# A linear-attention block and an MLP on one core: shorter warming, half of a block's reciprocal loads on ScalarE's queue, two more DMA transposes, and a new order

## The chip, the core and the metric

The kernel runs on one core of a Trainium2 chip. The core has TensorE (PE: matrix products, with its weight loads shown apart as PEld), VectorE (DVE), ScalarE (ACT), GpSimd (POOL) and SyncE (SP), which here only issues DMAs. Each engine works through its own queue in order, and semaphores between the queues make an instruction wait for what it reads or overwrites. Products land in PSUM, whose eight banks of 128 x 512 floats are one tile, `bk`.

The metric is device time in microseconds (us), median of several executions. The profile is of one execution, and its times count from the start of the profiled span.

## The reference, cut to what matters

All is bfloat16 outside; S = 2048 rows, D = 512, 32 heads of 16, Dff = 1792.

```python
n = layernorm(x)
q, k, v = split_heads(n @ wqkv)
phi = lambda t: where(t > 0, t + 1, exp(t)) + 1e-6
pq, pk = phi(q), phi(k)
kv = einsum("bhsd,bhse->bhde", pk, v)        # sums over all 2048 rows
z  = einsum("bhsd->bhd", pk)
o  = einsum("bhqd,bhde->bhqe", pq, kv) / (einsum("bhqd,bhd->bhq", pq, z)[..., None] + 1e-6)
h  = x + o_as_rows @ wo
out = h + maximum(layernorm(h) @ w1, 0) @ w2
```

`kv` and `z` need every row, so the attention's second half can't begin before the last row tile's `pk` is there.

## The kernel before

The 2048 rows are 16 row tiles of 128 (t), in 4 blocks of 512 columns after transposition (c = 0 to 3; c = 0 is block 1 of the title). The program is one list of words, `ORDER` (lines 18 to 54). Each word calls one small function, `op_<name>`, with the numbers behind the dots, and issues that function's instructions. Nothing else decides the order: an engine's queue is the list cut down to the words of that engine.

The words that matter here, by stage:

- `warm.n.b.w` (line 243): n products of zeros, w columns wide, before there is data.
- `lx`, `lk`, `lq`, `lv`, `lo`, `l1`, `l2`: loads of row tiles and weights, on SP. `l1` and `l2` of 896 KB bring the two halves of w1 and w2.
- `S.t`, `A.t` (lines 248, 249, DVE): statistics of row tile t; `R` (254, 255, ACT): the reciprocal root; `N.t` (262, DVE): the normalised rows.
- `T.t` (287, PE) transposes by four products, `E.t` (297, ACT) copies the result to `lnT`. For tiles 5 to 15 `X.t` (308, SP) does it with one DMA transpose.
- `K.t.b` (316, PE) is k of a row tile in bank b, four products of 512 columns; `K.t.b.k.n` does n of the four from k. `Q.c.j.b` (324, PE) is a quarter of q of block c. Behind either: exp (`F`, `qF`; line 334, ACT), relu (`U`, `qU`; 337, ACT), `M`/`qM` (341, DVE) and the addition `D`/`qD` (344, DVE).
- `G.t` (368, PE) sums n^T pk over the rows into banks 4 to 7; `za`, `zf`, `zhi`, `zlo` (DVE) sum pk, and `z` (392, PE) turns the sums to columns. The k of the last tiles goes straight into `z`, which so needs the last `D`.
- `zc`, `zh` (DVE), then `d4.c` (440, PE): the denominators of block c; `dl4`, `dx4` (446, 451, ACT): their reciprocals by log and exp. `wb.c` (468, SP) writes them to DRAM, and eight `rb.c.h` (471, SP; 64 KB each) read them back spread over the rows of one buffer, `rr`. `dm.c` (484, DVE) multiplies pq by them, into `pqs`.
- `gA`, `gD` (406, 409) copy the sums G out; `kv` (414, PE), `kx` (422, DVE, into `kvbd`), `m` (426, PE), `mA`, `mD` (429, 432): the weights of the second half, `m_sb`.
- `h.t` (493, PE), `hD.t` (499, DVE): h of a row tile, with the residual. `s`, `a` (250, 251, DVE): its statistics; `n.t` (270, DVE) or `nA.t` (276, ACT) subtracts the mean (with the sign turned); then `x.t` (309, SP) transposes by DMA. Tiles 2 and 3 have instead `t.t` (287, PE) and `v.t` (306, DVE).
- `p.c.f` (508, PE): 128 columns of the hidden layer for a block, four products; `ph.c.f.b.half` (517) the same for half of the block's rows; `pA`/`pD` (523, 528) the relu. `f.t.b.f0.n` (537, PE) the last products of a row tile, `fo` (545, DVE) the sum with h, `fd` (552, SP) the store.

Two rules set waits in all stages: a bank is overwritten only when its readers are through, and `rr`, `eb` and `rb` are used again in the same way.

Of the kernel before, what the change touches and what calls it, by code (L numbers as in the profile page):

```python
# [15 lines left out]


ORDER = """
table const masks warm.70.7.64 warm.2.7 lx.0.1 S.0 A.0 R.0.1 lx.1.1 S.1 lx.2.1 A.1 N.0 T.0.1 lk.0.4 S.2 R.1.1
N.1 T.1.2 lx.3.1 A.2 E.0 K.0.4 R.2.1 lx.4.2 S.3 N.2 T.2.1 E.1 A.3 S.5 R.3.1 K.1.0.0.2 K.1.0.2.2 N.3 S.4 A.5 A.4  # L20
E.2 T.3.2 K.2.6.0.2 K.2.6.2.2 F.0.1 M.0.1 lx.6.2 E.3 S.7 lq.0.4 R.4.2 lx.8.4 Q.0.3.1 N.4 U.0.1 A.7 F.1.1 F.2.1
T.4.2 N.5 S.6 Q.0.1.4 U.1.1 M.1.1 A.6 lx.12.4 M.2.1 D.0.1 R.6.2 K.3.7.0.2 K.3.7.2.2 E.4 X.5 U.2.1 U.3.1 D.1.1
N.6 Q.0.0.3 N.7 S.10 qF.0.0.2 K.4.5 K.5.6 S.8 A.10 S.9 A.8 qU.0.0.2 S.12 F.4.2 D.2.1 X.6 Q.0.2.0 A.9 A.12 K.6.2
S.13 S.11 M.4.2 A.11 A.13 U.4.2 D.4.2 F.3.1 R.8.2 N.9 M.3.1 X.7 K.7.3 R.12.2 R.10.2 N.8 F.6.2 D.3.1 N.13 S.15
G.0 G.1 U.6.2 S.14 X.9 X.8 N.10 A.14 A.15 N.12 qM.0.0.2 M.6.2 X.13 qF.0.2.2 R.14.2 qU.0.2.2 qM.0.2.2 N.11 G.2
G.3 G.5 G.4 N.14 X.12 K.9.3 K.8.2 K.13.1 N.15 qD.0.0.2 D.6.2 za.4.1 X.11 X.10 F.8.2 U.8.2 M.8.2 K.12.0 U.12.2
F.12.2 G.7 za.6.0 K.11.3 D.8.2 qD.0.2.2 M.12.2 za.8.0 K.10.2 F.10.2 X.14 G.8 K.14.0 U.10.2 X.15 K.15.1 M.10.2 zf
lv.2.2 lv.0.2 G.9 D.10.2 zhi D.12.2 F.14.2 G.6 G.10 G.11 M.14.2 zlo U.14.2 D.14.2 z.0.0 z.2.0 z.3.0 z.1.0 G.14
lo.0.2 lo.2.2 zc zh d4.0.1 dl4.0 l1.0.2 G.13 G.12 G.15 dx4.0 gA.2.2 Q.1.1.3 Q.1.0.2 qF.1.0.2 gD.0.2 kv.1.4
kv.3.4 kv.0.4 kv.2.4 kx qU.1.0.2 qM.1.0.2 qD.1.0.2 Q.1.3.1 Q.1.2.0 qF.1.2.2 m.0.2 m.1.3 mD.0.2 m.3.7 m.2.6 wb.0  # L30
Q.2.0.4 Q.2.1.5 rb.0.7 rb.0.1 rb.0.6 rb.0.3 rb.0.0 rb.0.2 rb.0.4 rb.0.5 l1.2.2 qM.1.2.2 qU.1.2.2 Q.2.3.1
qD.1.2.2 mA.2.2 qF.2.0.2 Q.2.2.0 qU.2.0.2 dm.0.2.2 dm.0.0.2 qM.2.0.2 h.1.6 hD.1 s.1 a.1 qU.2.2.2 d4.1.3 dl4.1
h.0.7 hD.0 s.0 dx4.1 h.2.6 h.3.5 a.0 l2.0.7 wb.1 hD.2 nA.1 hD.3 qF.2.2.2 nA.0 s.2 s.3 Q.3.0.2 Q.3.1.3 a.2
Q.3.3.6 a.3 qF.3.0.2 qU.3.0.2 Q.3.2.5 x.1 r.0.4 qF.3.2.2 n.2 t.2.7 n.3 t.3.4 qD.2.0.2 v.2 v.3 x.0 ph.0.3.1.0
ph.0.1.3.0 ph.0.2.0.0 ph.0.3.1.1 qM.2.2.2 qM.3.0.2 ph.0.0.2.0 ph.0.0.2.1 qM.3.2.2 qD.3.0.2 qU.3.2.2 qD.2.2.2
ph.0.2.0.1 qD.3.2.2 p.0.7.5 d4.2.6.2 pD.0.2.2 dl4.2 dl4.3 rb.1.4 rb.1.6 rb.1.3 rb.1.2 rb.1.0 rb.1.1 ph.0.1.3.1
rb.1.7 rb.1.5 p.0.6.4 dx4.2 dm.1.0.2 dm.1.2.2 h.4.0 pD.0.0.2 hD.4 pD.0.6.2 p.0.5.1 h.6.6 dx4.3 p.0.4.0 hD.6
l2.7.7 h.5.4 pA.0.4.2 s.4 s.6 hD.5 h.7.7 a.4 a.6 p.0.11.6 p.0.10.5 s.5 hD.7 a.5 p.0.9.4 wb.2 rb.2.6 n.4 rb.2.0
rb.2.4 s.7 n.6 rb.2.3 rb.2.2 rb.2.1 a.7 n.5 n.7 rb.2.5 rb.2.7 dm.2.0.2 dm.2.2.2 pD.0.10.2 p.0.13.1 p.0.12.0
p.0.8.3 pD.0.12.2 wb.3 r.4.4 rb.3.0 rb.3.4 h.10.7 hD.10 x.6 h.8.2 h.11.6 hD.8 s.10 rb.3.5 rb.3.1 rb.3.6  # L40
f.1.0.0.7 rb.3.3 rb.3.2 rb.3.7 s.8 hD.11 pD.0.8.2 h.9.5 f.3.1.0.7 x.7 x.5 s.11 a.8 hD.9 f.1.0.7.7 f.0.4.0.7 a.10
a.11 x.4 dm.3.2.2 dm.3.0.2 h.14.7 h.12.3 s.9 n.11 h.15.6 a.9 n.10 h.13.2 fo.1 n.9 n.8 hD.14 s.14 hD.12 x.11
hD.15 f.0.4.7.7 r.8.4 p.1.13.7 p.1.6.3 a.14 hD.13 s.12 s.15 s.13 a.12 a.15 a.13 n.14 p.1.12.6 n.13 f.3.1.7.7
n.12 n.15 p.1.2.5 fo.0 pD.1.12.2 x.10 p.1.7.4 fo.3 p.1.3.6 x.9 pD.1.6.2 pD.1.2.2 r.12.4 x.8 p.1.11.2 p.1.10.1
pD.1.10.2 f.2.4.0.7 p.2.0.6 p.2.1.7 f.2.4.7.7 pD.2.0.2 p.2.10.0 p.2.11.1 fo.2 x.14 p.2.6.2 p.2.7.3 x.15 fd.3
p.2.13.7 p.2.12.6 pD.2.10.2 pD.2.6.2 x.12 fd.1 pD.2.12.2 p.2.2.0 x.13 fd.0 p.2.3.1 p.1.5.6 p.1.4.5 pD.2.2.2
pD.1.4.2 p.1.0.3 p.1.1.4 p.1.9.1 p.1.8.0 pD.1.0.2 pD.1.8.2 f.4.4.0.7 f.4.4.7.7 fo.4 fd.4 f.5.3.0.7 f.5.3.7.7
fo.5 fd.2 f.6.7.0.7 f.6.7.7.7 fo.6 p.2.4.2 p.2.5.3 f.7.0.0.7 f.7.0.7.7 pD.2.4.2 fo.7 p.3.6.1 p.3.7.2 pD.3.6.2
p.3.8.3 p.3.9.4 p.3.5.1 pD.3.8.2 p.3.4.0 pD.3.4.2 fd.6 p.3.10.3 p.3.11.4 pD.3.10.2 p.3.2.0 p.3.3.1 p.3.0.5
p.3.1.6 pD.3.2.2 pD.3.0.2 p.3.13.3 fd.7 p.3.12.2 pD.3.12.2 f.10.1.0.7 f.15.2.0.14.3.1 f.15.7.0.14.0.2 p.2.8.4  # L50
p.2.9.5 fo.15.3.1 fd.15.3.1 fo.15.0.2 pD.2.8.2 f.8.7.0.7 f.10.1.7.7 fo.10 f.8.7.7.7 fo.8 f.14.2.0.7 f.14.2.7.7
f.13.3.0.7 fd.5 fd.8 fd.10 fo.14 f.13.3.7.7 fo.13 f.9.0.0.7 f.9.0.7.7 fd.15.0.2 f.11.6.0.7 f.11.6.7.7 fd.13 fo.9
f.12.0.0.7 fd.9 f.12.0.7.7 fo.11 fd.14 fd.11 fo.12 fd.12 f.15.2.0.14.2.1 fo.15.2.1 fd.15.2.1
"""


# [1 line left out]
def kernel(  # L58
# [253 lines left out]
    def op_K(t, b, k=0, n=KD):  # L312
        c, j = divmod(t, CT)
        at_bank["k", t] = b
        for kd in range(k, k + n):
            nc.tensor.matmul(  # L316
                bk[:, b, :], lhsT=lnT[c][:, kd, j * P : (j + 1) * P], rhs=wk_sb[:, kd, :],
                start=(kd == 0), stop=(kd == KD - 1),
            )
# [147 lines left out]
    def op_wb(c):  # L467
        nc.sync.dma_start(out=scr[c].rearrange("j h o n -> (j h) (o n)"), in_=rd[:, c, :])

    def op_rb(c, h):  # L470
        nc.sync.dma_start(
            out=rr[h * DH : (h + 1) * DH, :, :],
            in_=scr[c][:, h, :, :].rearrange("j o n -> o j n").broadcast_to([DH, KD, CW]),
        )
# [113 lines left out]
```

## Time and profile before

| | |
|---|---|
| median of 3 runs | 169.89 us (169.71 to 170.19) |
| span of the profiled execution | 168.0 us, 1.89 less than the median |
| PE busy | 162.7 us, 97% |
| DVE busy | 115.6 us, 69% |
| ACT busy | 49.5 us, 29% |
| POOL busy | 4.8 us, 3% |
| moved by DMA | 16.01 MB, mean 95 GB/s |
| granted PE clock | 1.00 |

A busy share is an average over stages with different limits. What sets the time is read from the chain of work that ended last: the profile follows it back from the last instruction, at each step to what released it or to the instruction ahead of it on its engine. In timelines each row is a group of merged instructions: start, length, engine, line, operation, what it writes and reads, count, and in brackets the idle time of the engine ahead of it and who ended it. Consecutive instructions of an engine overlap, so their spacing is less than their length: four products of 512 columns last 1.03 us together, and the next four start 0.86 us after the first.

### The profile page before, as it was taken

Reading aid. Unit: us, or ns where it says so; the run is one execution under the profiler, and the core shown is the slowest. Engines: PE = TensorE matmul, PEld = TensorE weight load, DVE = VectorE, ACT = ScalarE, POOL = GpSimd, SP = SyncE. Lnnn points to the kernel's source line nnn. Section 1 sums busy time; section 2 is a strip of 40 time slices with the busy share of each in tenths; the row PEclk is TensorE's granted clock in tenths of the full one; section 3 lists DMA queues with packets and bytes.
Section 4 is the critical chain, followed back from the end, with each engine's and each line's share of the span. In section 5 each row is a group of like instructions: output and inputs, shape, how many; then the busy total and the mean of one; then the engine's idle time right before and its main releaser. Section 6 shows DMA issues by size and latency. Waiting matters only on the chain.

```text
span 168.0 us, 2417 instructions
## 1 busy us (share of the span) xinstructions
PE 162.7 (97%) x924; PEld 79.2 (47%) x924; DVE 115.6 (69%) x217; ACT 49.5 (29%) x83; POOL 4.8 (3%) x21
## 2 busy tenths in 40 slices
...
GB/s 108 353 298 88 20 106 95 189 301 45 132 337 161 98 205 132 132 48 123 83 102 57 126 63 0 0 0 0 62 31 35 0 0 7 32 34 48 31 94 39
DMA packets 25003, 16.01 MB, mean 95 GB/s; under 512 B 15008, under 2 KB 23968, under 8 KB 24992
## 3 DMA queue, kind: packets, MB, share of 16 engines
...
q8 instruction: 7, 0.11, 0.3%
q14 instruction: 4, 0.03, 0.1%
...
## 4 chain that ended last, share of the span: by engine, by line
PE 92%; DMA 4%; SPq 2%; DVE 1%; issue 0%
PE bk L537 28%; PE bk L508 27%; PE bk L324 8%; PE bk L368 8%; PE bk L493 8%; PE bk L316 7%; DMA wq_sb<-in_A_wqkv_dram 4%; PE bk L517 2%; SPq L214 2%; PE bk L440 1%; DVE gT L545 1%; PE bk L392 1%; PE bk L414 1%; PE bk L426 1%; PE bk L287 0%
## 5 line engine op out<-in xcount | busy, mean ns | idle before, releaser
L537 PE MATMUL bk<-w_sb,at 128*128 128x512 bf16 (+2 forms) x252 | 50.0, 355 | 0.0
L508 PE MATMUL bk<-lnT,w_sb 128*128 128x512 bf16 x208 | 46.9, 379 | 0.0
L528 DVE TENSOR_SCALAR at<-bk 128x1024 bf16<-128x1024 f32 x27 | 32.8, 1223 | 13.2 <-PE bk L508 13.2
L537 PEld LDWEIGHTS <-at 128*128 128x128 bf16 x252 | 23.5, 98 | 25.4
L508 PEld LDWEIGHTS <-w_sb 128*128 128x128 bf16 x208 | 20.4, 98 | 23.9
L545 DVE SCALAR_TENSOR_TENSOR gT<-bk,rstd,h_nat 128x512 bf16<-128x512 f32 (+2 forms) x18 | 12.4, 691 | 24.6 <-PE bk L537 22.0
L334 ACT ACTIVATE eb<-bk 128x1024 bf16<-128x1024 f32 (+1 forms) x18 | 16.6, 929 | 5.3 <-PE bk L316 2.8
L337 ACT ACTIVATE rb<-bk 128x1024 bf16<-128x1024 f32 (+1 forms) x18 | 16.4, 929 | 0.0
L324 PE MATMUL bk<-lnT,wq_sb 128*128 128x512 bf16 x64 | 15.1, 379 | 0.3 <-DMA wq_sb<-in_A_wqkv_dram 0.3
L316 PE MATMUL bk<-wk_sb,lnT 128*128 128x512 bf16 x64 | 15.3, 379 | 0.0
L493 PE MATMUL bk<-m_sb,pqs 128*128 128x512 bf16 x64 | 15.1, 379 | 0.0
L368 PE MATMUL bk<-at,h_nat 128*128 128x512 bf16 x56 | 13.1, 379 | 0.0
L248 DVE BATCH_NORM_STATS2 st<-x_nat 128x6 f32<-128x512 bf16 x16 | 10.6, 678 | 2.3 <-DMA x_nat<-in_A_x_dram 2.3
L499 DVE TENSOR_TENSOR h_nat<-bk,x_nat 128x512 bf16<-128x512 f32 x16 | 10.6, 676 | 0.9 <-PE bk L493 0.9
L254 ACT ACTIVATE rstd<-mv,eps 128x2 f32<-128x2 f32 (+2 forms) x14 | 4.2, 297 | 23.7 <-DVE mv L251 20.9
L250 DVE BATCH_NORM_STATS2 st<-h_nat 128x6 f32<-128x512 bf16 x16 | 10.5, 684 | 0.1
L324 PEld LDWEIGHTS <-wq_sb 128*128 128x128 bf16 x64 | 6.1, 98 | 7.7 <-DMA wq_sb<-in_A_wqkv_dram 0.8
L493 PEld LDWEIGHTS <-pqs 128*128 128x128 bf16 x64 | 6.1, 98 | 7.7 <-DVE pqs L484 0.6
L368 PEld LDWEIGHTS <-h_nat 128*128 128x128 bf16 x64 | 6.1, 98 | 7.3 <-issue 0.2
L316 PEld LDWEIGHTS <-lnT 128*128 128x128 bf16 x64 | 6.1, 98 | 6.8
L341 DVE TENSOR_SCALAR eb<-eb 128x1024 bf16<-128x1024 bf16 (+1 forms) x18 | 6.6, 389 | 0.0
L262 DVE TENSOR_SCALAR h_nat<-x_nat,mv,rstd 128x512 bf16<-128x512 bf16 x16 | 6.3, 408 | 0.2 <-ACT rstd L255 0.2
...
## 6 DMA issues: line engine op xcount, KB each, us to landing
w_sb<-in_B_w_dram SPq DMA_DIRECT2D x4, 896.0 KB, 6.2
rr<-scr SPq DMA_DIRECT2D x32, 64.0 KB, 2.6
...
```

The lines of the kernel that those rows point to most:

```text
L248: op_S = lambda t: nc.vector.bn_stats(out=st[:, t, :], in_=x_nat[:, t, :])
L316: nc.tensor.matmul(bk[:, b, :], lhsT=lnT[c][:, kd, j * P : (j + 1) * P], rhs=wk_sb[:, kd, :], start=(kd == 0), stop=(kd == KD - 1),)
L324: nc.tensor.matmul(bk[:, b, :], lhsT=wq_sb[:, kd, j * P : (j + 1) * P], rhs=lnT[c][:, kd, :], start=(kd == 0), stop=(kd == KD - 1),)
L334: nc.scalar.activation(out=buf(eb, kind, i, n), in_=bank(at_bank[kind, i], n), func=ACT.Exp)
L337: nc.scalar.activation(out=buf(rb, kind, i, n), in_=bank(at_bank[kind, i], n), func=ACT.Relu)
L368: nc.tensor.matmul(bk[:, KD + kd, :], lhsT=ln_nat[:, t, kd * P : (kd + 1) * P], rhs=pk(t)[:, 0, :], start=(not stated), stop=(len(stated) ...
L493: nc.tensor.matmul(bk[:, b, :], lhsT=pqs[:, (c * KD + jb) % NQ, j * P : (j + 1) * P], rhs=m_sb[:, jb, :], start=(jb == 0), stop=(jb == KD ...
L499: nc.vector.tensor_tensor(out=h_nat[:, t : t + n, :], in0=bank(at_bank["h", t], n), in1=x_nat[:, t : t + n, :], op=ALU.add,)
L508: nc.tensor.matmul(bk[:, b, :], lhsT=w1_sb[:, kd, f * P : (f + 1) * P], rhs=lnT[c][:, kd, :], start=(kd == 0), stop=(kd == KD - 1),)
L528: nc.vector.tensor_scalar(out=acts[c % 2][:, f : f + n, :], in0=bank(at_bank["p", c, f], n), scalar1=-1.0, scalar2=0.0, op0=ALU.mult, op1= ...
L537: nc.tensor.matmul(bk[:, b, 0 : w * P], lhsT=acts[c % 2][:, f, j * P : (j + 1) * P], rhs=w2_sb[:, f, k * P : (k + w) * P], start=(f == 0), ...
L545: nc.vector.scalar_tensor_tensor(out=o_t[:, t % NO, cols], in0=bk[:, at_bank["f", t, k], 0 : w * P], scalar=rstd2[:, t : t + 1], in1=h_nat ...
```

## The change

It does four things.

- `warm.70.7.64` becomes `warm.35.7.128`: half as many products, of twice the width.
- Of block 1's eight reciprocal loads four stay on SP (`rb.0.0`, `.2`, `.4`, `.6`) and four are issued by ACT (`ab.0.1`, `.3`, `.7`, `.5`), between `gA.2.2` and `qF.1.0.2`.
- Tiles 2 and 3 of the second norm are transposed by DMA (`x.2`, `x.3` on SP, ahead of `wb.1`); `t.2`, `t.3`, `v.2` and `v.3` go.
- The whole list is put in a new order, from a plan that reckons with averaged landing times of the DMAs. A row tile's products may now be fed in any order, so `part` counts them and marks the first and the last.

In the new order the statistics of tiles 0, 1 and 2 come before the first `N`; `K.3` stands ahead of `Q.0`; the loads after the DMA transposes are `lv.2.2`, `l1.2.2`, `lo`, `lo`, `lv.0.2`; the `h` of block 1 stand ahead of six `Q` (before, four); and `l2.7.7` follows the four loads left on SP.

```diff
@@ ORDER @@
-table const masks warm.70.7.64 warm.2.7 lx.0.1 S.0 A.0 R.0.1 lx.1.1 S.1 lx.2.1 A.1 N.0 T.0.1 lk.0.4 S.2 R.1.1
-N.1 T.1.2 lx.3.1 A.2 E.0 K.0.4 R.2.1 lx.4.2 S.3 N.2 T.2.1 E.1 A.3 S.5 R.3.1 K.1.0.0.2 K.1.0.2.2 N.3 S.4 A.5 A.4
-E.2 T.3.2 K.2.6.0.2 K.2.6.2.2 F.0.1 M.0.1 lx.6.2 E.3 S.7 lq.0.4 R.4.2 lx.8.4 Q.0.3.1 N.4 U.0.1 A.7 F.1.1 F.2.1
-T.4.2 N.5 S.6 Q.0.1.4 U.1.1 M.1.1 A.6 lx.12.4 M.2.1 D.0.1 R.6.2 K.3.7.0.2 K.3.7.2.2 E.4 X.5 U.2.1 U.3.1 D.1.1
...
-F.12.2 G.7 za.6.0 K.11.3 D.8.2 qD.0.2.2 M.12.2 za.8.0 K.10.2 F.10.2 X.14 G.8 K.14.0 U.10.2 X.15 K.15.1 M.10.2 zf
-lv.2.2 lv.0.2 G.9 D.10.2 zhi D.12.2 F.14.2 G.6 G.10 G.11 M.14.2 zlo U.14.2 D.14.2 z.0.0 z.2.0 z.3.0 z.1.0 G.14
-lo.0.2 lo.2.2 zc zh d4.0.1 dl4.0 l1.0.2 G.13 G.12 G.15 dx4.0 gA.2.2 Q.1.1.3 Q.1.0.2 qF.1.0.2 gD.0.2 kv.1.4
-kv.3.4 kv.0.4 kv.2.4 kx qU.1.0.2 qM.1.0.2 qD.1.0.2 Q.1.3.1 Q.1.2.0 qF.1.2.2 m.0.2 m.1.3 mD.0.2 m.3.7 m.2.6 wb.0
-Q.2.0.4 Q.2.1.5 rb.0.7 rb.0.1 rb.0.6 rb.0.3 rb.0.0 rb.0.2 rb.0.4 rb.0.5 l1.2.2 qM.1.2.2 qU.1.2.2 Q.2.3.1
-qD.1.2.2 mA.2.2 qF.2.0.2 Q.2.2.0 qU.2.0.2 dm.0.2.2 dm.0.0.2 qM.2.0.2 h.1.6 hD.1 s.1 a.1 qU.2.2.2 d4.1.3 dl4.1
-h.0.7 hD.0 s.0 dx4.1 h.2.6 h.3.5 a.0 l2.0.7 wb.1 hD.2 nA.1 hD.3 qF.2.2.2 nA.0 s.2 s.3 Q.3.0.2 Q.3.1.3 a.2
-Q.3.3.6 a.3 qF.3.0.2 qU.3.0.2 Q.3.2.5 x.1 r.0.4 qF.3.2.2 n.2 t.2.7 n.3 t.3.4 qD.2.0.2 v.2 v.3 x.0 ph.0.3.1.0
-ph.0.1.3.0 ph.0.2.0.0 ph.0.3.1.1 qM.2.2.2 qM.3.0.2 ph.0.0.2.0 ph.0.0.2.1 qM.3.2.2 qD.3.0.2 qU.3.2.2 qD.2.2.2
-ph.0.2.0.1 qD.3.2.2 p.0.7.5 d4.2.6.2 pD.0.2.2 dl4.2 dl4.3 rb.1.4 rb.1.6 rb.1.3 rb.1.2 rb.1.0 rb.1.1 ph.0.1.3.1
-rb.1.7 rb.1.5 p.0.6.4 dx4.2 dm.1.0.2 dm.1.2.2 h.4.0 pD.0.0.2 hD.4 pD.0.6.2 p.0.5.1 h.6.6 dx4.3 p.0.4.0 hD.6
-l2.7.7 h.5.4 pA.0.4.2 s.4 s.6 hD.5 h.7.7 a.4 a.6 p.0.11.6 p.0.10.5 s.5 hD.7 a.5 p.0.9.4 wb.2 rb.2.6 n.4 rb.2.0
...
+table const lx.0.1 warm.35.7.128 lx.1.1 masks lx.2.1 lk.0.4 lx.3.1 S.0 lx.4.2 S.1 lx.6.2 lq.0.4 A.0 A.1 warm.2.7
+S.2 R.1.1 lx.8.4 R.0.1 lx.12.4 A.2 N.1 R.2.1 N.0 T.1.7 N.2 T.0.0 E.1 T.2.3 E.0 K.1.7.2.2 S.3 E.2 K.1.7.0.2 A.3 S.5
+K.0.5 R.3.1 U.1.1 N.3 S.4 F.1.1 T.3.2 K.2.3.0.2 E.3 A.4 K.2.3.2.2 M.1.1 A.5 U.0.1 S.6 K.3.6.2.2 R.4.2 K.3.6.0.2
+S.7 F.0.1 Q.0.0.4 N.4 F.3.1 M.0.1 D.1.1 U.2.1 Q.0.2.0 M.3.1 A.7 N.5 F.2.1 A.6 D.0.1 X.5 T.4.7 R.6.2 Q.0.1.5 S.8
...
+qM.0.2.2 G.5 N.12 U.6.2 N.13 A.14 X.12 qD.0.0.2 G.4 F.6.2 S.10 G.3 S.11 X.13 R.14.2 qU.0.2.2 K.8.2 M.6.2 A.11 A.10
+N.14 R.10.2 D.6.2 K.9.3 X.14 N.15 G.7 N.10 F.8.2 za.4.1 X.15 K.13.1 U.8.2 M.8.2 K.12.0 X.10 N.11 za.6.0 K.14.2
+U.12.2 X.11 D.8.2 K.15.3 F.12.2 za.8.0 lv.2.2 G.8 F.14.2 l1.2.2 qD.0.2.2 K.10.0 lo.0.2 U.14.2 lo.2.2 M.14.2 K.11.1
+zf lv.0.2 D.14.2 G.6 F.10.2 M.12.2 zhi G.9 D.12.2 U.10.2 M.10.2 G.15 zlo G.12 D.10.2 z.2.3 z.3.3 z.1.3 z.0.3 G.10
+zc zh d4.0.3 G.11 dl4.0 dx4.0 G.13 wb.0 G.14 Q.1.0.2 gA.2.2 gD.0.2 rb.0.0 Q.1.1.3 ab.0.1 rb.0.2 ab.0.3 rb.0.4
+kv.3.6 kv.0.6 ab.0.7 rb.0.6 kv.2.6 kv.1.6 ab.0.5 l2.7.7 Q.2.1.1 kx qF.1.0.2 l1.0.2 m.0.4 m.1.5 qU.1.0.2 m.3.7
+mD.0.2 Q.2.0.0 m.2.6 Q.1.2.2 dm.0.2.2 mA.2.2 dm.0.0.2 Q.1.3.3 qF.2.0.2 qM.1.0.2 qD.1.0.2 h.1.4 qU.1.2.2 qM.2.0.2
+h.0.5 hD.1 qU.2.0.2 h.2.7 s.1 qF.1.2.2 hD.0 h.3.0 a.1 s.0 nA.1 Q.2.2.4 a.0 hD.2 x.1 nA.0 Q.3.0.1 qM.1.2.2 s.2
+Q.3.1.2 x.0 hD.3 a.2 Q.2.3.5 n.2 qF.3.0.2 s.3 x.2 Q.3.3.7 qU.3.0.2 a.3 n.3 qD.1.2.2 Q.3.2.6 x.3 qF.2.2.2 qM.3.0.2
+d4.1.3 ph.0.2.0.0 qM.2.2.2 dl4.1 qD.3.0.2 ph.0.0.2.0 dx4.1 ph.0.3.1.0 ph.0.1.3.0 qU.2.2.2 wb.1 ph.0.3.1.1
+ph.0.2.0.1 qF.3.2.2 qD.2.2.2 ph.0.0.2.1 qD.2.0.2 ph.0.1.3.1 qU.3.2.2 p.0.11.5 rb.1.2 pD.0.2.2 rb.1.7 p.0.10.4
+rb.1.3 qM.3.2.2 rb.1.6 qD.3.2.2 p.0.12.6 rb.1.0 pD.0.10.2 rb.1.4 d4.2.0.2 rb.1.5 p.0.13.7 dl4.2 rb.1.1 r.0.4
+p.0.5.5 pD.0.12.2 dx4.2 dl4.3 p.0.4.4 wb.2 l2.0.7 p.0.8.1 dm.1.0.2 pA.0.4.2 dm.1.2.2 p.0.7.7 dx4.3 pD.0.0.2 rb.2.4
...
+rb.3.4 rb.3.0 h.10.2 hD.9 rb.3.6 a.4 rb.3.5 h.11.5 s.6 rb.3.7 a.7 fo.0 f.3.7.0.7 rb.3.1 rb.3.3 hD.10 rb.3.2
+f.2.1.7.7 fo.3 a.6 s.9 h.8.0 n.6 n.7 n.4 x.7 hD.11 f.1.3.0.7 dm.3.0.2 x.6 s.10 f.1.3.7.7 fo.2 x.4 a.9 a.10
+dm.3.2.2 h.14.6 s.11 fd.2 h.12.1 hD.14 fo.1 h.13.5 hD.8 p.1.1.4 hD.12 p.1.12.2 s.8 n.10 p.1.13.3 s.14 x.10 a.11
+n.11 h.15.1 n.9 a.8 fd.1 pD.1.12.2 r.8.4 p.1.7.7 fd.3 r.4.4 x.9 hD.15 p.1.6.6 s.15 p.1.9.3 fd.0 pD.1.6.2 x.11
...
@@ -169,6 +169,12 @@
     z_on = lambda n: z_sb.rearrange("p (k o) -> p k o", o=1).broadcast_to([P, KD, n])
     at_bank = {}
     summed, stated = set(), set()
+    fed = {}
+
+    def part(key, n):
+        at = fed[key] = fed.get(key, 0) + 1
+        return {"start": at == 1, "stop": at == n}
+
     dsts = {"k": lambda t, n: pk(t, n), "q": lambda i, n: pqT[i // KD][:, i % KD : i % KD + n, :]}
     unit = {"k": 0, "q": NT}
 
@@ -315,7 +321,7 @@
         for kd in range(k, k + n):
             nc.tensor.matmul(
                 bk[:, b, :], lhsT=lnT[c][:, kd, j * P : (j + 1) * P], rhs=wk_sb[:, kd, :],
-                start=(kd == 0), stop=(kd == KD - 1),
+                **part(("k", t), KD),
             )
 
     def op_Q(c, j, b):
@@ -467,11 +473,14 @@
     def op_wb(c):
         nc.sync.dma_start(out=scr[c].rearrange("j h o n -> (j h) (o n)"), in_=rd[:, c, :])
 
-    def op_rb(c, h):
-        nc.sync.dma_start(
+    def spread(eng, c, h):
+        eng.dma_start(
             out=rr[h * DH : (h + 1) * DH, :, :],
             in_=scr[c][:, h, :, :].rearrange("j o n -> o j n").broadcast_to([DH, KD, CW]),
         )
+
+    op_rb = lambda c, h: spread(nc.sync, c, h)
+    op_ab = lambda c, h: spread(nc.scalar, c, h)
 
     def op_rs(c, j):
         rows = rd[j * Q4 : j * Q4 + P // DH, c, :]
@@ -537,7 +546,7 @@
             nc.tensor.matmul(
                 bk[:, b, 0 : w * P], lhsT=acts[c % 2][:, f, j * P : (j + 1) * P],
                 rhs=w2_sb[:, f, k * P : (k + w) * P],
-                start=(f == 0), stop=(f == KF - 1),
+                **part(("f", t, k), KF),
             )
 
     def op_fo(t, k=0, w=KD):
```

33 lines of the change are left out of this document (14 added, 19 removed).

## The prediction

> **What bounds the kernel now.** I read the page's chain first, then the chain in order of time, then the busy time by stages, then the timelines around the places where the change moves waits.
>
> ```profile
> span 168.0 us, 2417 instructions
> ...
> PE 92%; DMA 4%; SPq 2%; DVE 1%; issue 0%
> ```
> ```profile
> 4.16 6.17 DMA wq_sb<-in_A_wqkv_dram
> ...
> 10.38 1.04 PE bk L324 x4
> ...
> 37.67 0.33 PE bk L440 x4
> ...
> 56.70 0.45 PE bk L287 x8
> 57.15 3.06 PE bk L517 x28
> ...
> 164.22 0.77 DVE gT L545
> ```
> ```profile
> 10.40:35.60 25.20, 25.20 (x120) 11.56 (x121) 24.47 (x60) 20.74 (x34) 0.00 (x0) 1.00 0.50 125
> ...
> 40.70:49.20 8.50, 8.50 (x53) 4.30 (x51) 6.13 (x10) 7.08 (x8) 0.00 (x0) 1.00 0.57 179
> ...
> 62.90:100.00 37.10, 37.10 (x174) 16.72 (x173) 33.98 (x66) 3.39 (x9) 0.00 (x0) 1.00 0.40 99
> 100.00:164.20 64.20, 64.20 (x319) 30.27 (x318) 29.45 (x30) 0.00 (x0) 0.00 (x0) 1.00 0.07 25
> ```
>
> The chain is TensorE (PE) from 10.38 to 164.22, and every stage row has PE busy for its whole length. So only three things can move the time: what PE has behind it when it becomes continuous, the amount of PE work after that, and any wait that opens. VectorE (DVE) is nearly as full until 35.6 (24.47 of 25.20) and from 62.9 to 100 (33.98 of 37.10).
>
> The sum is made against the profiled span, 168.0. The median, 169.89, is 1.89 above it; I add that at the end.
>
> **The start.** The loads keep their order. The fourth row tile still lands at 6.6. These are rows of the timeline (start, length, engine, line; in brackets the idle time ahead and its releaser).
>
> ```profile
> 1.05 4.08 PE L245 MATMUL bk<-m_sb 128*128 128x64 bf16 x72 [1.05 <-DVE m_sb L186]
> ...
> 3.03 0.69 DVE L248 BATCH_NORM_STATS2 st<-x_nat 128x6 f32<-128x512 bf16 x1 [1.79 <-DMA x_nat<-in_A_x_dram]
> ...
> 5.09 0.40 PE L287 MATMUL bk<-ident,h_nat 128*128 128x128 bf16 x4
> ...
> 6.08 0.40 PE L287 MATMUL bk<-ident,h_nat 128*128 128x128 bf16 x4 [0.59 <-DVE h_nat L262]
> ...
> 6.62 0.69 DVE L248 BATCH_NORM_STATS2 st<-x_nat 128x6 f32<-128x512 bf16 x1 [0.51 <-DMA x_nat<-in_A_x_dram]
> ...
> 8.32 0.41 DVE L262 TENSOR_SCALAR h_nat<-x_nat,mv,rstd 128x512 bf16<-128x512 bf16 x1
> ...
> 9.02 1.03 PE L316 MATMUL bk<-wk_sb,lnT 128*128 128x512 bf16 x4
> ...
> 9.22 0.60 ACT L297 ACTIVATE lnT<-bk 128x512 bf16<-128x512 bf16 x1
> ```
>
> Warming: the columns stay 4,480. If PE pays by columns (70 products in some 3.5 us here), they end at the same time and the edit costs nothing: PE then waits for the first normalised tile anyway. If it paid by instruction they would end near 2.9; the first tile would still set the next start. A halved clock could cost up to the 1.7 us of two projections (four products each, 0.86), but idle gaps of 0.59 show clock 1.00. A gain is excluded, since the tile is what PE waits for. I take zero.
>
> Statistics of tiles 0, 1 and 2 now run ahead of the first normalisation, so N.1 starts at 5.3 (before, N.0 did at 4.65) and the first transpose at 5.74 instead of 5.09. That lateness is absorbed: three transposes, K.1 (from 6.97), K.0, T.3 and K.2 follow without a gap to 9.81, while tile 3 keeps its chain from landing: statistics 6.62, N.3 8.3, transpose 8.7, copy E.3 to 9.8, PE 0.2 later. So K.3 starts at 9.98, ends issuing at 10.85, and Q.0 follows; wq landed at 10.33. Before, the same set (T.0 to T.3, K.0 to K.2) was done at 10.38 and K.3 came later, which makes it 11.24 for the equal set. Gain 0.40. Its bounds: 0 if tile 3 is 0.4 later, 0.45 by the next row.
>
> **Does DVE let it stand?** The state column sums (z, L392) need DVE's last addition.
>
> ```profile
> 34.39 0.69 DVE L344 TENSOR_TENSOR at<-rb,eb 128x1024 bf16<-128x1024 bf16 x1
> ...
> 35.65 0.19 PE L392 MATMUL bk<-ones,zhl 128*128 128x1 bf16 x2
> ```
>
> DVE's last addition ended at 35.08 and z started at 35.65. DVE's operations until then are the same in number and kind, and there was hardly a gap to close; so z can start at about 35.2 and no earlier. Of the 0.40 I count 0.05 as lost here.
>
> **Transposes of tiles 2 and 3.** Two PE transposes and their two copies go.
>
> ```profile
> 57.03 0.75 DVE L306 COPY lnT<-bk 128x512 bf16<-128x512 bf16 x2
> ```
>
> The chain's row at 56.70 gives PE 0.45 less. DVE saves 0.75, which by itself gains nothing: PE doesn't wait for DVE in this stage.
>
> Their place is taken by two DMA transposes on SP, with n.2 and n.3 ahead of them. In what follows I keep the clock of before (shift it by the gain).
>
> ```profile
> L309 SPq DMA_TRANSPOSE lnT<-hn x14: 1188/1206/1277, 52.7 to 95.3; - x14
> ...
> DMA to landing us min/median/max: 2.4/2.4/3.0
> ```
> ```profile
> 49.20 1.03 PE L493 MATMUL bk<-m_sb,pqs 128*128 128x512 bf16 x4
> ...
> 55.92 0.60 DVE L270 TENSOR_SCALAR hn<-h_nat,mv 128x512 bf16<-128x512 bf16 x2
> ```
>
> Before, n.3 ended 7.3 after h.1 began. In the new order h.1 begins at 47.6, because two Q products (1.73) move behind the h's; n.3 then ends near 55.5 (0.5 later relative to h.1, for qM.1.2 and n.2 stand before it). Its transpose lands 2.4 later, at 57.9. PE meanwhile does four h and six Q (0.86 each, 8.64), d4.1 (0.33, the chain's row at 37.67) and four half groups of four products (0.109 each by the chain's row at 57.15, 1.74): the first that needs tile 3 starts at 58.36. Cover 0.4; if a landing takes the 3.0, 0.2 is lost. On SP the two issues (1.21 each) stand ahead of wb.1, which waits for dx4.1 until 58.1 anyway.
>
> **Reciprocal loads.** This is what makes room for the earlier h.1.
>
> ```profile
> 39.43 0.34 SPq L468 DMA_DIRECT2D scr<-rd  x1
> ...
> 40.53 1.89 PE L324 MATMUL bk<-lnT,wq_sb 128*128 128x512 bf16 x8
> ...
> 40.73 1.02 ACT L406 ACTIVATE gT<-bk 128x1024 bf16<-128x1024 f32 x1 [1.33 <-PE bk L368]
> ...
> 41.17 3.62 SPq L471 DMA_DIRECT2D rr<-scr  x8
> ...
> 42.26 1.06 PE L414 MATMUL bk<-gT,wv_sb 128*128 128x128 bf16 x16
> ...
> 42.46 1.02 ACT L334 ACTIVATE eb<-bk 128x1024 bf16<-128x1024 f32 x1 [0.70 <-PE bk L324]
> ...
> 43.35 0.69 DVE L422 TENSOR_TENSOR kvbd<-bk,mask 128x512 bf16<-128x512 f32 x1 [1.82 <-PE bk L414]
> ...
> 43.38 1.02 ACT L337 ACTIVATE rb<-bk 128x1024 bf16<-128x1024 f32 x1
> ...
> 45.51 1.23 DVE L432 CAST m_sb<-bk 128x1024 bf16<-128x1024 f32 x1 [0.34 <-PE bk L426]
> ...
> 47.78 1.29 DVE L484 TENSOR_TENSOR pqs<-pqT,rr 128x1024 bf16<-128x1024 bf16 x2
> ```
> ```profile
> w_sb<-in_B_w_dram SPq DMA_DIRECT2D x4, 896.0 KB, 6.2
> rr<-scr SPq DMA_DIRECT2D x32, 64.0 KB, 2.6
> ```
>
> Eight issues took 3.62, 0.45 each. The last began at 44.36 and by the median of 2.6 landed near 46.96. With four on each queue the last begins at 42.55 and lands at 45.15. PE from 40.53: Q.1.0, Q.1.1, kv, Q.2.1, which ends issuing at 44.02; then m.0 needs kvbd, which DVE gives at 44.05 (43.35 + 0.69): with 0.08 to load it, PE waits 0.1. Before, a second Q covered this. Then m.0, m.1, m.3, Q.2.0, m.2 bring Q.1.2 to 45.86 and h.1 to 47.6. h.1 needs both dm products, 1.29 long, so the loads must have landed by 46.2: cover 1.0. From it I take up to half, since the 896 KB load now follows four issues and not eight, and shares the DMA engines with ScalarE's last loads. mD.0 frees DVE at 45.9.
>
> On ScalarE (ACT) the four issues stand behind gA.2.2 and ahead of qF.1.0. No row shows an issue by ACT, so its length c is open. At SP's 0.45 they end at 42.98 and the exp and relu of bank 2 and 3 (starts 0.92 apart, the second 1.02) are through at 44.96. Q.1.2 overwrites bank 2 at 45.86: cover 0.9. The cover is gone at c = 0.66, and each 0.1 above costs 0.4. The low end of c is zero (nothing gained, the cover only grows), the high end the 1.21 of a transposing issue. I take 0.45, the same instruction on another queue.
>
> ```profile
> L471 SPq DMA_DIRECT2D rr<-scr x32: 303/424/529, 41.2 to 77.8; - x32
> ```
>
> No DMA_DIRECT2D of this form took more than 0.53. The Trainium skill (Perfetto Trace Analysis, section DMA Instruction — HWDGE) speaks against this: the block that generates descriptors is one, shared by the two issuing sequencers, and locked for each DMA, with the wait for the lock inside the profiled interval. By that rule alone the two queues would take turns and c would come to about 0.9; no run so far shows two queues at once.
>
> **The rest of the new order.** Later places with little cover: the c=1 loads (wb.1 at 58.1, last landing 66.2, dm.1 done 67.5, h.5 on PE 67.57); h.14's second half, which DVE's dm.3.2 meets at 88.8 against 88.7. I count 0.1 for these. From 100 on DVE has 34.75 us of room, and the tail behind the last product keeps its operations.
>
> **Sum.** -0.40 (start) + 0.05 (z) - 0.45 (transposes) + 0.10 (m.0) + 0.10 (late places) = -0.60. 168.0 - 0.6 + 1.89 = 169.3.
>
> **Rivals.**
>
> *Shared issue.* The two queues take turns, c = 0.9, ACT's issues end with SP's at 44.34 to 44.79, and bank 2 is through at 46.3 to 46.75. Q.1.2 waits 0.5 to 0.95; the loads land near 46.96 as before, in time for the later h.1. Then -0.60 + 0.7 = +0.1: 170.0. For it: SP's issues follow each other without a gap at 0.45, as they would if one full unit made them. Against: no row shows that any of the 0.45 is spent in a part that both queues use. (This is where the Trainium skill's rule above leads.)
>
> *ACT held long (the other sign).* Place: L334's exp of Q.1 behind the four issues. Price: 0.4 for each 0.1 of c above 0.66. At c = 0.81 all gain is gone; slower by over 0.3% from c = 0.94. At 1.21, Q.1.2 waits 2.2: -0.6 + 2.2 = +1.6, 171.5. For it: SP's transposes show issues of that length. Against: the form is that of L471.
>
> *The start doesn't gain.* DVE, full to 24.47 of 25.20, slips by 0.4 at any of its waits on exp, and z starts at 35.6 as before: -0.45 + 0.2 = -0.25, 169.65.
>
> *Late landings.* The 896 KB load delays ACT's last loads past 46.2 by 1.2 (the rows of such loads reach 6.2 for the load itself): h.1 waits 1.2, +0.6, 170.5.
>
> **How the numbers follow.** Forecast 0.55, shared issue 0.12, ACT held 0.13, no gain at the start 0.10, late landings 0.10. About 0.3% (0.5 us) is what a measurement of this kernel can tell from no change. Faster: 169.38 or less is four fifths of the forecast (0.44), and 0.01 from the start rival: 0.45. Same: 0.11 of the forecast, 0.09 each of shared issue and the start rival: 0.29. Slower: ACT held 0.13, late landings 0.10, 0.03 of shared issue: 0.26. The likeliest case by itself spans 169.0 (all 0.85 kept) to 169.7 (stalls of 0.6). The range runs from 168.9, the most that start and transposes can give, to 170.7, leaving out ACT held.
>
> **What would show it.** Right: PE continuous from about 10, K.3 ahead of Q.0; z's first product near 35.2; eight fewer L287 products; ACT's issues of 0.4 to 0.5 each and no idle PE before L324 between 45 and 47. Wrong: PE idle released by ACT L337 before a Q, by DMA through L484 before L493, or by DMA before L517; a granted clock under 1.00 after 5.

## The result and the profile after

The changed kernel takes 171.03 us (median; 170.53 to 171.47) against 169.84 of the kernel before on the same chip: a ratio of 1.0078, 95% interval 1.0056 to 1.0100. It is slower by 0.8%. The profiled execution has a span of 169.3 against 168.0. The forecast was 169.3, with a range up to 170.7.

First the profile's page of the changed kernel: its span, the shares of the chain that ended last, and the rows of the four DMA queues (packets, MB, share of 16 engines).

```profile
span 169.3 us, 2311 instructions
...
q1 hardware_dynamic: 25760, 15.87, 34.3%
q10 hardware_dynamic: 320, 0.26, 0.8%
q8 instruction: 7, 0.11, 0.3%
q14 instruction: 4, 0.03, 0.1%
...
PE 69%; DVE 13%; DMA 8%; SPq 3%; issue 2%; ACT 1%; ACTq 1%; DVEq 0%
```

Before, PE made up 92% of that chain. Now it leaves PE for DMA and DVE in several places: PE waits somewhere. The view of PE's waits in the changed kernel says where (line waited at, releaser: total us, times, longest):

```profile
PE bk L526 <- DMA lnT<-hn: 1.3, 1, 1.3
PE bk L251 <- DVE m_sb L192: 1.0, 1, 1.0
PE bk L293 <- DVE h_nat L268: 0.8, 1, 0.8
PE bk L502 <- DVE pqs L493: 0.3, 1, 0.3
```

The first row is new, and so is the small last one. Before 6 us PE waited in the old kernel too; the 1.3 us on a transpose of the second norm did not exist there. (L526 is `ph`, L517 of the old numbering.) The chain in order of time around it, changed kernel:

```profile
54.84 0.35 DVE hn L276
55.20 0.10 DVE pqT L350
55.30 4.07 DMA lnT<-hn
59.37 0.04 issue
59.41 1.91 PE bk L526 x16
```

This is `x.3`, issued at 55.30 (the forecast had 55.5, on the old kernel's clock). It landed 4.07 us later and not 2.4. The busy times by stage (stretch; length, PE, PEld, DVE, ACT, POOL, clock, DMA share, GB/s) confine the loss: in the third row PE is busy 4.22 of 5.50, and nowhere else after the start is more than 0.7 missing. The granted clock is 1.00 in all.

```profile
10.40:35.00 24.60, 24.49 (x119) 11.29 (x120) 24.26 (x60) 20.17 (x33) 0.00 (x0) 1.00 0.53 147
40.70:47.10 6.40, 6.34 (x40) 3.06 (x39) 3.35 (x6) 3.99 (x5) 0.00 (x0) 1.00 0.83 206
55.90:61.40 5.50, 4.22 (x39) 3.35 (x39) 3.47 (x6) 4.41 (x6) 0.00 (x0) 1.00 0.27 70
63.00:100.00 37.00, 36.37 (x172) 16.21 (x174) 30.77 (x56) 4.61 (x11) 0.00 (x0) 1.00 0.44 102
```

Why did this one transpose take 1.7 longer than its neighbours? The DMA rows of the stretch from 55 to 60 us in the changed kernel hold something besides the kernel's own transfers:

```profile
q1 hardware_dynamic: 1232, 0.39, 34.7%
q8 instruction: 1, 0.02, 1.2%
...
lnT<-hn SPq DMA_TRANSPOSE x2, 3.2
```

One packet of 16 KB on queue q8, "instruction". The page shows seven of them in the whole run. In the trace they come each time TensorE has taken some 125 more products (each a weight load and a product), so I read them as fetches of TensorE's own program. The packets of the trace at this place (start in us, ns taken, bytes):

```
57.17 to 57.37   30 packets of x.3, 4 bytes, 7 to 9 ns each
57.36            q8: 931 ns, 16384 bytes (ends 58.29)
58.27, 58.28     the last 2 of x.3's 32 packets of 4 bytes, 24 and 21 ns
59.37            x.3 counts as landed
```

Thirty of the 32 closing packets (those of 4 bytes, which follow the transpose's data) went at once; two went out only when the fetch was through. The working theory: **halving the warming products takes 70 instructions out of TensorE's program, all later fetches come at other moments, and one now falls on `x.3`.** The rival: the new order or the wider products cost the time, and the fetch is a bystander.

### The profile page after: what moved, and what is told of

It is laid out like the page before. It is cut to its first block, busy times and chain, and to the rows that moved or that the text cites. A ratio compares the mean times of both kernels' runs of the same rounds, so it can differ in the third digit from the quotient of the medians.

```text
span 169.3 us, 2311 instructions
## 1 busy us (share of the span) xinstructions
PE 161.7 (95%) x865; PEld 78.4 (46%) x881; DVE 115.1 (68%) x215; ACT 49.4 (29%) x83; POOL 4.7 (3%) x21
## 4 chain that ended last, share of the span: by engine, by line
PE 69%; DVE 13%; DMA 8%; SPq 3%; issue 2%; ACT 1%; ACTq 1%; DVEq 0%
PE bk L517 25%; PE bk L546 21%; PE bk L322 8%; PE bk L374 7%; DMA rr<-scr 4%; PE bk L502 3%; DVE h_nat L508 2%; DMA lnT<-hn 2%; SPq L477 2%; DVE st L256 2%; DVE pqs L493 2%; PE bk L330 2%; DVE at L537 1%; DMA x_nat<-in_A_x_dram 1%; PE bk L526 1%
## 5 line engine op out<-in xcount | busy, mean ns | idle before, releaser
L517 PE MATMUL bk<-lnT,w_sb 128*128 128x512 bf16 x206 | 46.9, 379 | 0.1
L517 PEld LDWEIGHTS <-w_sb 128*128 128x128 bf16 x208 | 20.3, 98 | 24.5 <-issue 0.4
L350 DVE TENSOR_TENSOR pqT<-rb,eb 128x1024 bf16<-128x1024 bf16 x8 | 5.4, 684 | 1.5 <-ACT rb L343 1.3
```

Source lines behind the costliest of these rows:

```text
L517: nc.tensor.matmul(bk[:, b, :], lhsT=w1_sb[:, kd, f * P : (f + 1) * P], rhs=lnT[c][:, kd, :], start=(kd == 0), stop=(kd == KD - 1),)
```

## The experiments

**Undo the warming edit alone.**

```diff
-table const lx.0.1 warm.35.7.128 lx.1.1 masks
+table const lx.0.1 warm.70.7.64 lx.1.1 masks
```

> The changed kernel with its warming put back to 70 products of 64 columns, all else as changed. Fetch theory: TensorE's own instructions come in 16 KB DMA packets of about 0.93 us (one at 57.36, one at 80.25 in the changed kernel's trace), each when TensorE has used up a fixed count of instructions; 35 products more at the start bring each packet 35 products earlier, to about 52 and 73. Then x.3 lands 2.4 after its issue (changed kernel: 4.07), the first load of the fourth block's reciprocals issues in about 0.4 (1.53), TensorE's wait for the transposed rows (1.3) goes, and the wait before h.14 (0.5) goes: 1.9 less, about 169.2, 0.4% under the kernel before. Rival, four transposes in a row with a write behind them: x.3 lands after 4 as it did, and the time stays at 171.0. Rival, the narrow warming is slower or faster by itself: the first transpose starts at another time than 5.66.

Measured: 169.34 us (169.24 to 169.61), ratio to before 0.9973 (0.9953 to 0.9994). PE's waits and the transposes of the second norm issued from 51 to 60 us, in this kernel:

```profile
PE bk L251 <- DVE m_sb L192: 1.1, 1, 1.1
PE bk L293 <- DVE h_nat L268: 0.3, 1, 0.3
```
```profile
L315 SPq DMA_TRANSPOSE lnT<-hn x4: 1188/1206/1217, 51.5 to 55.4; - x4
...
DMA to landing us min/median/max: 2.4/2.4/2.4
```

After the start PE waits for nothing of note. All four transposes land in 2.4. The fetch ran from 50.43 to 51.63, over when the first of them, issued at 51.47, had just begun. So the change without its warming edit comes near what was forecast for the whole: 0.4 us under the kernel before in the same set of runs (169.72), where 0.6 was forecast. The edit that the forecast put at zero costs 1.7 us here.

**The warming edit in the kernel before.**

```diff
-table const masks warm.70.7.64 warm.2.7 lx.0.1
+table const masks warm.35.7.128 warm.2.7 lx.0.1
```

> The kernel before with only the warming changed, 35 products of 128 columns. Fetch theory: the packets come 35 products later than before's 35.55, 51.41 and 71.03, at about 42, 57 and 78.5; there the DMAs under way are reciprocal loads and a transpose with 1 to 4 us of cover, so the time stays within 0.3% of 169.8. By the rival that the wider warming costs something by itself at the start: the first transpose later than 5.09, and the loss of the changed kernel (1.2) shows here too.

Missed: 171.09 us (170.04 to 171.72), ratio 1.0079 (1.0046 to 1.0112). The edit costs 1.4 us in the old order as well, at another place. The first transpose starts where it did (5.07 against 5.09), so the width does no harm at the start. But a fetch ran from 58.03 to 59.20, and the chain in order of time, in this kernel, has this:

```profile
57.73 0.42 SPq L471
...
58.20 1.36 SPq L471
...
60.08 2.67 DMA rr<-scr
...
62.88 0.70 DVE pqs L484
```

One reciprocal load's issue took 1.36 where its neighbours take 0.42 to 0.44; the last loads landed later, and `h.4` put PE 0.52 further behind, waiting for `dm.1` (61.80 was the last landing before, 62.75 here). It is 0.69 with the second half of `h.4`, which started another 0.18 late. An earlier fetch, from 14.20 to 15.35, met a transpose of the first norm, which landed in 3.75, and put PE 0.35 behind at a `K`. Less the 0.09 by which this execution was ahead, that is the 0.95 between the profiled spans (168.90 and 167.95). What was expected counted on covers of 1 to 4 us; it left out that a fetch also holds an issue, and with it every load behind.

**All eight reciprocal loads on SP.**

```diff
-rb.0.0 Q.1.1.3 ab.0.1 rb.0.2 ab.0.3 rb.0.4
+rb.0.0 Q.1.1.3 rb.0.1 rb.0.2 rb.0.3 rb.0.4
@@
-ab.0.7 rb.0.6 kv.2.6 kv.1.6 ab.0.5
+rb.0.7 rb.0.6 kv.2.6 kv.1.6 rb.0.5
```

> The changed kernel with all eight loads of the first block's reciprocals on SP, in the same order. If the split is worth what its cover says: the eight issues take 3.6 from 40.48, the last lands near 46.6 instead of 45.61, dm.0 starts 0.9 to 1.0 later than 45.79, h.1 waits that much more, and the time is 0.8 to 1.0 above the changed kernel's 171.0, unless it is taken up by the wait for x.3 (then the same). Rival, ScalarE's issues cost more than they bring: the time falls by up to 0.5, Q.1.2 starts earlier.

Measured: 172.27 us (172.03 to 172.82), ratio 1.0151 (1.0115 to 1.0188), 1.2 us above the changed kernel, a little more than the 0.8 to 1.0 expected. PE's waits, and the first `h` on its timeline:

```profile
PE bk L502 <- DVE pqs L493: 1.7, 2, 1.0
PE bk L526 <- DMA lnT<-hn: 1.3, 1, 1.3
```
```profile
48.31 3.63 PE L502 MATMUL bk<-m_sb,pqs 128*128 128x512 bf16 x16 [0.70 <-DVE pqs L493]
```

The split helps the earlier `h`: without it `h.1` starts 0.86 late and with it 0.22, so it is worth 0.64 there. The other 1.0 of the 1.7 stands at `h.14`, where the changed kernel waits 0.3, and isn't the split's: the fetch at 81.25 took 1.68 there (1.21 in the changed kernel) and held a load's issue for 1.85 (1.53). So the 1.2 is not the price of the split alone. The wait on `x.3` is untouched, with a fetch at 58.51, 1.2 later as everything is. So neither the split nor ScalarE's part in it makes the loss.

**A number in between.**

```diff
-table const lx.0.1 warm.35.7.128 lx.1.1 masks
+table const lx.0.1 warm.53.7.84 lx.1.1 masks
```

> The changed kernel with 53 warming products of 84 columns (4452 columns, as many as before within 1%). Fetch theory: the packets come 18 products earlier than in the changed kernel, at about 55.6 (beside x.2, which has cover, ahead of x.3) and 77 (between the loads and x.5): x.3 lands by 57.9, no wait for it, no wait before h.14, about 169.2. Rival, four transposes in a row: x.3 lands after 4 and the time stays at 171.0.

Missed: 171.08 us (170.85 to 171.38), ratio 1.0077 (1.0050 to 1.0104). The fetch did not move by 18 products; it came at 57.72 and met `x.3` again:

```profile
PE bk L526 <- DMA lnT<-hn: 1.5, 1, 1.5
```

The next fetch did move, from 80.25 to 76.73, and the late landing of `x.5` and the wait of `h.14` went with it. So the number of products shifts the fetches, but not one for one: by the weight loads begun at that moment the third fetch came at 339 to 363 in the kernels of this study. The second hardly moved in time, 36.20 with 35 products, 36.20 with 53, 35.50 with 70 and 34.46 with 80, and so came at 221 to 261 loads. What places a fetch within such a spread, 24 products or some 5 us of PE work for the third, isn't settled. The miss rules out one tempting reading, though: that 35 products or their width is special.

**The width kept, the number restored.**

```diff
-table const lx.0.1 warm.35.7.128 lx.1.1 masks
+table const lx.0.1 warm.30.7.128 warm.40.7.16 lx.1.1 masks
```

> The changed kernel with 70 warming products again, now 30 of 128 columns and 40 of 16 (the same 4,480 columns; most of them by wide products). If it is the number of TensorE's instructions that puts the fetch of its instructions on x.3's transpose, the fetch is near 50 to 52 us, x.3 lands 2.4 us after its issue and the time is 169.3 to 169.6. If the width of the warming products is the cause, x.3's late landing and the time of the changed kernel, 171.0, stay.

Measured: 169.66 us (169.41 to 170.34), ratio 1.0001 (0.9989 to 1.0013). Most columns come from wide products, the number is 70, and the loss is gone: fetch at 50.69, all four transposes 2.4. It is the count and not the width. (The kernel with 80 products, below, took 169.42 in the same set of runs; no wait of PE after the start explains these 0.2.)

**Take away what the fetch hits.** Tile 3 goes back to TensorE; 35 products stay.

```diff
-x.3 qF.2.2.2 qM.3.0.2 d4.1.3 ph.0.2.0.0 qM.2.2.2 dl4.1 qD.3.0.2 ph.0.0.2.0
+qF.2.2.2 qM.3.0.2 d4.1.3 ph.0.0.2.0 t.3.0 v.3 qM.2.2.2 dl4.1 qD.3.0.2
@@
-dx4.1 ph.0.3.1.0 ph.0.1.3.0 qU.2.2.2
+ph.0.3.1.0 dx4.1 ph.0.1.3.0 ph.0.2.0.0 qU.2.2.2
```

> The changed kernel with tile 3 of the second norm transposed by TensorE again (four products into bank 0, copied by VectorE); tile 2 stays on DMA and there are 35 warming products. By the fetch theory the fetch is still near 57 us, but nothing that TensorE waits for is in flight then: the wait of 1.4 us goes, 0.22 us of products comes, and the time is 169.7 to 170.1. If the new order has another wait behind this one (the loads of block 2's reciprocals, say), TensorE waits there instead and the time stays at 170.6 to 171.1.

Measured: 169.94 us (169.53 to 171.20), ratio 1.0030 (1.0009 to 1.0051), as the fetch theory had it. The DMA rows from 55 to 60 us of this kernel still hold the fetch (at 57.97):

```profile
q8 instruction: 1, 0.02, 1.2%
...
scr<-rd SPq DMA_DIRECT2D x1, 128.0 KB, 1.8
lnT<-hn SPq DMA_TRANSPOSE x1, 2.4
```

The fetch is there, the wait isn't. So the fetch itself doesn't hold TensorE; it costs through the landing it delays. Its successor at 79.25 fell on `x.5`, which landed in 3.3; that cost no wait here.

**Both tiles on TensorE, 70 products.** This was to price the term of 0.45.

```diff
-x.2 Q.3.3.7 qU.3.0.2 a.3 n.3 qD.1.2.2 Q.3.2.6 x.3 qF.2.2.2 qM.3.0.2 d4.1.3
+Q.3.3.7 t.2.0 v.2 qU.3.0.2 a.3 n.3 qD.1.2.2 Q.3.2.6 qF.2.2.2 qM.3.0.2 d4.1.3
```

(with 70 products of 64 and `t.3.0 v.3` as above)

> The changed kernel with 70 warming products of 64 columns and both tiles 2 and 3 transposed by TensorE: it prices the part with the DMA transposes without the fetch on it. The prediction's term says 0.45 us above the 169.34 of the kernel with 70 warming products and DMA transposes, so 169.8. If those products were hidden in a wait, 169.3; if VectorE's copies open a wait, above 170.

Measured: 170.67 us (170.30 to 170.97), ratio 1.0058 (1.0041 to 1.0075). Slower than the 169.8 that the term would have given, and PE's waits show the placing at fault:

```profile
PE bk L501 <- DVE pqs L492: 0.5, 1, 0.5
PE bk L445 <- DVE pqT L349: 0.4, 1, 0.4
```

The copy `v.2` waited 0.75 for its transpose on DVE, ahead of `a.3`, `n.3` and `qD.1.2`, and `d4.1` waited for the last of these. The row of L501 is the reciprocal loads landing later in this execution (the last at 46.23, against 45.74 in the first kernel with 70 products). As a price for the term the run is worthless; the next has both copies behind `qD.1.2` (`x.2` goes here too, and the `ph` behind stand in another order):

```diff
-Q.3.2.6 x.3 qF.2.2.2 qM.3.0.2 d4.1.3 ph.0.2.0.0
+Q.3.2.6 qF.2.2.2 d4.1.3 t.2.0 t.3.1 v.2 v.3 qM.3.0.2
```

> As the kernel before in this study with both tiles on TensorE and 70 warming products, but VectorE's two copies stand behind the additions that the denominators of block 2 wait for (there the first copy, waiting for the transpose, held them up and TensorE waited 0.41). If the prediction's term is right, 0.45 us above the kernel with 70 warming products and DMA transposes: 169.7 to 169.9. If the DMA transposes gain nothing, 169.3 to 169.5; if VectorE is the bound here, 170.2 or more.

Measured: 169.56 us (169.32 to 170.14), ratio 0.9992 (0.9976 to 1.0008). This lies between the two times expected. The kernel with 70 products and DMA transposes ran beside it:

> The changed kernel with 70 warming products of 64 columns once more, on the chip on which the other runs: 169.2 to 169.6, ratio to before between 0.995 and 0.999. If the first result was a chip's own, the ratio is 1.000 or above.

Measured: 169.38 us (169.22 to 170.00), ratio 0.9984 (0.9968 to 1.0001). The DMA transposes gain about 0.2 by these medians, less than half of the 0.45; the two sets of times overlap, so this is not measured finely. The first experiment's time came again within 0.04.

**More products.**

```diff
-table const lx.0.1 warm.35.7.128 lx.1.1 masks
+table const lx.0.1 warm.80.7.56 lx.1.1 masks
```

> The changed kernel with 80 warming products of 56 columns, the same 4,480 columns. By the fetch theory the fetches come some 2 us ahead of those with 70 products, the one in question near 48 to 52 us where no DMA is waited for, the next near 72: 169.2 to 169.6. If 70 is only a lucky number, another landing is late and the time is 170 to 171.

Measured: 169.42 us (169.10 to 169.85), ratio 0.9976 (0.9959 to 0.9992). The fetch came at 50.60, no earlier than with 70, so the expected shift of 2 us failed as it did with 53; the time is right because no transfer with a short cover was in flight. A later fetch, at 97.97, did hold a transpose to 4.3, and PE didn't wait for it.

All runs of the new order together, with the fetches nearest to `x.3` and `x.5` and these transposes' times from issue to landing. They come from four sets of runs, not all on one chip. The kernel before took 169.84 in the set of the first row, 169.72 in that of "loads on SP only", 53 and 70, 169.71 in that of "70 again" and the last row, and 169.64 in that of the others:

| kernel | products | fetch, us | x.3 | fetch, us | x.5 | median, us |
|---|---|---|---|---|---|---|
| after | 35 x 128 | 57.36 | 4.1 | 80.25 | 3.9 | 171.03 |
| loads on SP only | 35 x 128 | 58.51 | 4.1 | 81.25 | 4.2 | 172.27 |
| 53 | 53 x 84 | 57.72 | 4.3 | 76.73 | 2.4 | 171.08 |
| tile 3 on PE | 35 x 128 | 57.97 | none | 79.25 | 3.3 | 169.94 |
| 70 | 70 x 64 | 50.43 | 2.4 | 74.18 | 2.4 | 169.34 |
| 70 again | 70 x 64 | 50.93 | 2.4 | 74.93 | 2.4 | 169.38 |
| mixed 70 | 30 x 128, 40 x 16 | 50.69 | 2.4 | 74.42 | 2.4 | 169.66 |
| 80 | 80 x 56 | 50.60 | 2.4 | 73.99 | 2.4 | 169.42 |
| both tiles on PE | 70 x 64 | 50.90 | none | 74.62 | 2.4 | 170.67 |
| the same, copies later | 70 x 64 | 50.41 | none | 72.78 | 2.4 | 169.56 |

Each landing in this table with a fetch inside it took 3.3 to 4.3; each without took 2.4. Smaller packets do it too: in the kernel with 70 products the only later transposes of the second norm that were slow, 2.7 and 3.3, are two of three issued from 84.9 to 87.8, and there a packet of 8 KB on the other instruction queue, q14, ran at 86.70. The twelve traces hold 315 DMA transposes. In 254 of them no packet of q8 or q14 ran between issue and landing, and none of these took over 2.7; of the other 61, 23 took 2.9 to 4.3. So the fetch is no bystander, but not every meeting costs: where it ended within 0.4 of the issue, or began in the last 0.2 before the landing, the transpose took 2.4 to 2.5. The versions with 70 and 80 products of 64 and 56 columns are the best ones: 0.2 to 0.3% under the kernel before, no more than the 0.3% called measurable in the prediction.

## Why the prediction was wrong, point by point

**Warming, taken as zero: this is the step that failed.** Its working asked whether PE pays by column or by instruction and when the first tile comes, and that part holds: the first transpose starts at 5.66 with 35 products and at 5.71 with 70. What it left out is that 70 fewer instructions (35 products and their weight loads) move the later fetches of TensorE's program, the third by 6.9 us and the fourth by 6.1 here. The term was +1.7 (171.03 against 169.34; by the ratios 1.0078 against 0.9973), not 0. The prediction named "PE idle released by DMA" before `ph` as the sign that it is wrong, and that is the sign that appeared; the cause behind it was not among the rivals.

**The start, -0.40: right in direction, uncertain in size.** The changed kernel's PE timeline:

```profile
8.58 0.40 PE L293 MATMUL bk<-ident,h_nat 128*128 128x128 bf16 x4
8.82 1.89 PE L322 MATMUL bk<-wk_sb,lnT 128*128 128x512 bf16 x8
10.54 1.89 PE L330 MATMUL bk<-lnT,wq_sb 128*128 128x512 bf16 x8
```

K.2 and K.3 run without a gap and Q.0 starts at 10.54, 0.3 ahead of the forecast's 10.85. Taking PE's work off its clock, PE is 0.70 ahead of the kernel before here. But in the other profiled executions of this order T.3, the fourth tile's transpose, began between 8.67 and 9.26, as its row tile landed sooner or later (its statistics start at 6.59 in the changed kernel, at 7.28 in the one with 80 products); at 9.24, with 70 products again, the gain was 0.05. The prediction gave that bound ("0 if tile 3 is 0.4 later").

**The column sums, no earlier than 35.2: the bound was too late.** DVE's last addition, the first product of the sums and the first that needs this addition, changed kernel:

```profile
34.02 0.68 DVE L350 TENSOR_TENSOR at<-rb,eb 128x1024 bf16<-128x1024 bf16 x1
...
34.94 0.19 PE L398 MATMUL bk<-ones,zhl 128*128 128x1 bf16 x2
...
35.04 0.29 PE L398 MATMUL bk<-ones,at 128*128 128x1 bf16 x6
```

The last addition ended at 34.70, 0.38 earlier than before (35.08), so DVE had more of a gap to close than the prediction allowed. The first product came at 34.94, the part that needs this addition at 35.04, and nothing waited: not even the 0.05 was lost.

**Transposes, -0.45, and the cover of 0.4 behind `x.3`.** Without the fetch the cover held in all four kernels that show it. With it, a landing 1.7 late met a cover of 0.4, and PE's wait of 1.3 is the difference. The bound used for a late landing, 3.0, was the longest of the old kernel's second norm, and that one had itself met a packet: issued at 80.81, with 8 KB on q14 at 82.02. In the first norm a transpose issued at 11.10 had taken 3.42 with a q8 fetch from 11.43 to 12.51. So the old trace already held the collision that the sum left out. The term itself is smaller than forecast by the medians (0.2).

**ACT's issues, c = 0.45, and the rivals on it.** The rows of the loads in the changed kernel, over the whole run, and then the timeline of both issuing engines:

```profile
L477 SPq DMA_DIRECT2D rr<-scr x28: 313/422/1535, 40.5 to 84.7; - x28
...
L477 ACTq DMA_DIRECT2D rr<-scr x4: 317/402/438, 40.5 to 42.1; - x4
```
```profile
40.48 1.74 SPq L477 DMA_DIRECT2D rr<-scr  x4
```
```profile
40.48 1.98 ACTq L477 DMA_DIRECT2D rr<-scr  x4
42.51 1.02 ACT L340 ACTIVATE eb<-bk 128x1024 bf16<-128x1024 f32 x1 [1.46 <-PE bk L330]
```

ACT's issue takes 0.32 to 0.44, and both queues issue in the same 2 us: eight loads in 1.98 against 3.62 on SP alone. The exp behind them began at 42.51 and no Q waited. (The forecast's 42.98 is on the old clock, 0.7 behind this one at that place: `wb.0` was issued at 39.43 there and at 38.72 here.) So "ACT held long" is out, and so is "shared issue" as priced, with 0.9 for each of ACT's. Eight issues in 1.98 are 0.25 each, so a part of an issue up to that length could still be taken in turns; no run here shows whether it is. The rule of the Trainium skill on a locked descriptor generator (Perfetto Trace Analysis, section DMA Instruction — HWDGE) leads to 0.9 only if the whole of an issue is locked, and this trace shows that it isn't.

**The loads' landing, cover 1.0.** The forecast put the last landing at 45.15, less the 0.7 between the clocks 44.45; it came at 45.61, 1.2 late against a cover of 1.0. DVE's products ran from 45.79 to 47.08, and `h.1` waited 0.22. The DMA rows from 40 to 48 us, changed kernel first, then the kernel with all loads on SP, show why (KB each, median us to landing):

```profile
rr<-scr SPq DMA_DIRECT2D x4, 64.0 KB, 3.2
rr<-scr ACTq DMA_DIRECT2D x4, 64.0 KB, 3.4
```
```profile
rr<-scr SPq DMA_DIRECT2D x8, 64.0 KB, 2.6
```

Issued twice as fast, each load lands 0.6 to 0.8 later. The 896 KB load, issued at 43.05 and not at 44.65, has a part in the last ones that these runs don't separate; the second and third had landed by 43.84 and took 3.0 already. The late-landings rival had the place; its wait was 0.2 and not 1.2. Without the second queue (the kernel with all loads on SP) it was 0.9, so the split gave what the new order had already spent.

**The small waits.** `m.0` waited 0.17 (0.10 forecast). `h.14` put PE 0.50 further behind (0.33 of it idle by the timeline), waiting for `dm.3.2`; 0.10 was set aside for that and `h.5`. This has the same cause as `x.3`: with the fetch at 80.25, `x.5` landed in 3.9 and the load issued behind it took 1.53 to issue. With 70 products there is no such wait.

Added up on the profiled spans: -0.70 (start), -0.45 (work), +0.17, +0.22, +1.36 and +0.50 make +1.1; the spans differ by 1.4 (169.33 and 167.95). The remaining 0.3 isn't placed; missing product records blur the small gaps.
